# Nineteen attention units with three polynomial tiles in place of four, and the engines' orders written anew

## The chip, the cores and the metric

The kernel runs on one core of a Trainium2 chip, as one launch. The metric is the device time of that launch in microseconds (us). The profile is one execution on the chip, taken by the hardware profiler. A core has five engines that run their own instruction queues: PE (TensorE, matrix products into PSUM), ACT (ScalarE, here the exponentials), DVE (VectorE), POOL (GpSimd) and SP (SyncE, which issues most of the DMAs). Queues meet through semaphores alone, so an engine stands still as soon as the next instruction of its own queue has to wait.

## The reference, cut to what matters

Two independent attention blocks, each on 2,048 rows of 1,024 columns with 32 heads of 32 columns, in bfloat16. Their outputs stand side by side.

```python
def _A_ref(x, wqkv, wo):                    # branch A: full softmax attention
    q, k, v = ...                           # x @ wqkv, split in heads
    scores = einsum('bhqd,bhkd->bhqk', q, k) * Dh ** (-0.5)
    p = softmax(scores)
    o = einsum('bhqk,bhkd->bhqd', p, v)
    return o_joined @ wo

def _B_ref(x, wq, wk, wv, wo, beta):        # branch B: four segments of 512 rows
    for s in range(4):
        p = softmax(qs @ ks.T * scale + mask)   # inside the segment
        a_dot = p @ vs
        a_mem = (phi(qs) @ M) / (phi(qs) @ z + 1e-06)
        o = g * a_mem + (1.0 - g) * a_dot       # g = sigmoid(beta), by head
        M, z = M + phi(ks).T @ vs, z + phi(ks).sum()
    return o_joined @ wo                        # phi(t) = t + 1 if t > 0 else exp(t)
```

## The kernel before

**Units.** Branch A is cut into 64 units: a group of four heads (32 x 4 = 128 partitions) by 256 query rows. A unit has eight sets. A set is four score tiles of 128 x 512 (one for each head, two key blocks by 256 queries), made by PE at L1190 into four PSUM banks (`SLOT_BANKS`: three pairs of banks that rotate). Branch B has 16 units, each a pair of head groups in a segment, with five sets. The B units are dealt out between the A units.

**Exponentials.** A set's four tiles become P, bfloat16 in SBUF. Usually ACT does this with two instructions of 1,024 columns (two banks each), at L1288. So an A unit has 16 exponentials, a B unit ten. `P` is a ring of 20 tiles of 512 columns (`P_RING`). PE then multiplies P with V (L1401) and with a block of ones (L1408), which gives the output and the softmax's sums; DVE turns them (L1515), takes reciprocals (L1518), and POOL multiplies (L1526, L1533).

**Polynomial tiles.** The scores are small, so exp can be had from a parabola. In some sets of a unit the first head's tile does not go to ACT (`plan_cube`): DVE reads the score bank, scales and shifts it into Y (L1236, one of three buffers), POOL squares it into Z (L1245, one of two) and makes Pc from it (L1246, one of three). ACT's first exponential of such a set then has 512 columns in place of 1,024, and the set takes three slots of P in place of four. Which sets those are is said by a digit for each A unit in `POLYS`:

```python
POLYS = "4444444444444444444444444444444444444444444444444444444444444444"
CUBIC = {"3": (0, 2, 4), "4": (0, 2, 4, 6), "5": (0, 1, 2, 4, 6)}
...
        n = 8 * unit[1] + unit[2] if unit[1] < 6 else 48 + PAIR.index(unit[1:])
        return CUBIC[POLYS[n]]
```

The first four units have no polynomial tile, whatever their digit, and the last two have their own entry (`WHOLE`). Branch B uses the same Y, Z and parabola for phi (L1911, then L1245 and L1246, then L1925).

**Jobs.** Beside the units PE has projections (`mm4`, L829): keys, queries and values of later groups and segments, and the output products. `level` spreads them between their release and due times. DVE evicts them from PSUM (L1608) and squares keys and queries (L1621), from which a guard column is made that tells whether the parabola and the unshifted exp may be used; if not, ACT takes another branch of its program (`run_split`).

**Orders.** `schedule` places all operations by a list scheduler with written costs, which gives an order for each engine. `rearrange` then changes these orders by `MOVES`, a string for each engine: "3+2" goes three places on and pulls there the operation that stands two places later. `BANKS` says for each PSUM tenant (projections and sums) whether it lives in bank 6 or 7. Nothing but semaphores sets the time at run time: the written order is what each engine runs.

Of the kernel before, what the change touches and what calls it, by code (L numbers as in the profile page):

```python
# [25 lines left out]
    "666767676767666776766766676667666766676666676666766676666676767677666667666667676677676666766666766676766776766667666766"  # L26
    "666767676776666766667666676667666666666767676776666676666676666766667676677676667666667666666667676677676666766666667676"
    "766767666766667666766667666667666666667676767766666676666676666667676766776766676676666766766776766666766667666666676767"
    "677666676666676667666676667666666667677676676667667666666677676776766666766666667677767666766676676776776667666766667666"
    "66766667666667666677776"  # L30
# [13 lines left out]
POLYS = "4444444444444444444444444444444444444444444444444444444444444444"  # L44
# [101 lines left out]
class Op:  # L146
# [17 lines left out]
    def __hash__(self):  # L164
# [632 lines left out]
class _Kernel:  # L797
# [339 lines left out]
    def cubed(self, unit, part):  # L1137
# [5 lines left out]
        n = 8 * unit[1] + unit[2] if unit[1] < 6 else 48 + PAIR.index(unit[1:])  # L1143
        return CUBIC[POLYS[n]]

# [1139 lines left out]
```

## Time and profile before

| | |
|---|---|
| median of 3 runs | 1058.93 us (1058.56 to 1058.99) |
| profiled execution | 1057.97 us, its span 1056.3 us |
| PE busy | 1023.3 us, 97% of the span |
| ACT busy | 1001.5 us, 95% |
| POOL busy | 724.7 us, 69% |
| DVE busy | 703.4 us, 67% |
| granted TensorE clock | 1.000 |

The span runs from the first to the last instruction of the profile; the profiled execution's own time has 1.7 us around it. In the rows of groups, the text reads: line, engine, operation, what it writes and reads, shapes, count, then busy time in us and the mean of one in ns, then the engine's idle time before these instructions and what ended most of it. In the rows of stretches, each engine has its busy time in us and, in brackets, how many instructions run there; then come the granted clock, the share of the DMA engines and GB/s. In the rows of waits: who waited for whom, the total in us, how often, the longest. Records of successive exponentials overlap somewhat, so a row's mean is longer than the distance from one to the next.

### The profile page before, as it was taken

How to read it: one execution, taken by the hardware profiler on the slowest of the kernel's cores; microseconds unless marked ns; L12 is line 12 of the kernel's file. 1: busy time of each engine (PE TensorE's matmuls, PEld its weight loads, DVE VectorE, ACT ScalarE, POOL GpSimd, SP SyncE). 2: the span in 40 equal slices, each digit the busy share in tenths (PEclk: the TensorE clock that was granted, in tenths of full speed). 3: DMA queues.
4: the chain of work that ended last, by engine and by line, in shares of the span. 5: the costliest groups of instructions: out<-in, count | busy, mean ns of one | idle time of the engine just before them, and what ended most of it. 6: DMA issues, size and time to landing. Idle time of an engine off the chain costs nothing.

```text
span 1056.3 us, 54941 instructions
## 1 busy us (share of the span) xinstructions
PE 1023.3 (97%) x25091; PEld 551.2 (52%) x25092; DVE 703.4 (67%) x1451; ACT 1001.5 (95%) x1193; POOL 724.7 (69%) x999
## 2 busy tenths in 40 slices
PE   9999999999999999999999999999999999999998
PEld 4456455566555454556555445556555445445544
DVE  3457577666656878696755879777646887674444
ACT  5999999999999999898999999999999999999995
POOL 1005567666766888888956899888755878985551
PEclk9999999999999999999999999999999999999999
DMA  9213351007112530033241221133041433122002
GB/s 175 47 43 93 68 138 28 16 13 160 49 41 70 123 85 17 3 62 92 67 113 44 78 65 38 27 75 91 27 113 35 125 102 113 33 68 73 28 29 66
DMA packets 172377, 72.24 MB, mean 68 GB/s; under 512 B 135536, under 2 KB 170352, under 8 KB 172144
## 3 DMA queue, kind: packets, MB, share of 16 engines
q1 hardware_dynamic: 169776, 67.93, 26.3%
q8 instruction: 197, 3.23, 1.3%
q10 hardware_dynamic: 2368, 0.79, 0.3%
q14 instruction: 36, 0.29, 0.1%
HBM read 45.36 MB, written 11.80 MB: 54 GB/s over the span
## 4 chain that ended last, share of the span: by engine, by line
PE 56%; ACT 32%; DVE 4%; POOL 3%; SPq 3%; issue 1%; DMA 0%; ACTq 0%; POOLq 0%; DVEq 0%
ACT P L1288 32%; PE ps L829 27%; PE ps L1190 11%; PE ps L1401 8%; PE ps L1408 8%; SPq L1572 2%; POOL Z L1245 2%; DVE Y L1236 1%; PE ps L1866 1%; PE ps L1638 1%; POOL Pc L1246 1%; DVE T L1515 1%; DMA W_A<-in_A_wqkv_dram 0%; DVE PKQ_B L1925 0%; POOL P L1317 0%
## 5 line engine op out<-in xcount | busy, mean ns | idle before, releaser
L1288 ACT ACTIVATE P<-ps 128x1024 bf16<-128x1024 f32 (+1 forms) x1178 | 991.5, 999 | 33.6 <-PE ps L1190 18.7
L1245 POOL TENSOR_TENSOR Z<-Y 128x512 f32<-128x512 f32 x287 | 304.2, 1062 | 202.2 <-DVE Y L1236 177.7
L1408 PE MATMUL ps<-P,onesb 128*32 128x256 bf16 (+1 forms) x4386 | 300.8, 270 | 0.7 <-issue 0.6
L1401 PE MATMUL ps<-P,V_A 128*32 128x256 bf16 x3618 | 257.7, 274 | 0.7 <-issue 0.3
L1236 DVE TENSOR_SCALAR Y<-ps 128x512 f32<-128x512 f32 x239 | 163.7, 685 | 110.1 <-PE ps L1190 90.5
L1190 PE MATMUL ps<-KQ_A 32*128 32x256 bf16 x4096 | 204.1, 272 | 12.4 <-ACT P L1288 5.5
L1246 POOL TENSOR_SCALAR Pc<-Z 128x512 bf16<-128x512 f32 x239 | 155.6, 654 | 11.0 <-PE ps L1190 0.2
L1190 PEld LDWEIGHTS ps<-KQ_A 32*128 32x128 bf16 x4096 | 62.8, 92 | 163.9 <-ACT P L1288 108.7
L1408 PEld LDWEIGHTS ps<-P,onesb 128*32 128x32 bf16 x4386 | 128.8, 96 | 30.1 <-issue 14.8
L829 PE MATMUL ps<-xT_B,W_B 128*32 128x512 bf16 (+1 forms) x2132 | 138.7, 372 | 0.8 <-DVE OT_B L1948 0.2
L829 PE MATMUL ps<-xT_A,W_A 128*32 128x512 bf16 (+1 forms) x2020 | 131.4, 370 | 2.2 <-DMA W_A<-in_A_wqkv_dram 1.1
L1401 PEld LDWEIGHTS ps<-P,V_A 128*32 128x32 bf16 x3618 | 108.1, 96 | 34.3 <-issue 14.3
L1401 PE MATMUL ps<-Pc,V_A 128*32 128x256 bf16 x478 | 123.1, 273 | 0.4 <-ACT P L1288 0.2
L1408 PE MATMUL ps<-Pc,onesb 128*32 128x256 bf16 x478 | 122.8, 273 | 0.0
L1317 POOL TENSOR_SCALAR_AFFINE_SELECT P<-P 128x768 bf16<-128x768 bf16 (+1 forms) x96 | 76.3, 803 | 34.7 <-ACT P L1288 33.1
L1515 DVE STREAM_TRANSPOSE T<-ps 128x512 f32<-128x512 f32 x122 | 86.3, 708 | 14.0 <-PE ps L1408 11.9
L829 PEld LDWEIGHTS ps<-xT_B,W_B 128*32 128x32 bf16 x2132 | 50.3, 96 | 45.5 <-issue 19.6
L829 PE MATMUL ps<-Wo_B,OT_B 128*32 128x512 bf16 (+1 forms) x1080 | 71.6, 370 | 0.2 <-DVE rc L1518 0.2
L829 PE MATMUL ps<-Wv_B,xT_B 128*32 128x512 bf16 (+1 forms) x1096 | 70.3, 367 | 0.2
L829 PEld LDWEIGHTS ps<-xT_A,W_A 128*32 128x32 bf16 x2020 | 47.4, 96 | 42.1 <-issue 12.5
L1533 POOL TENSOR_TENSOR T<-T,rc 128x256 bf16<-128x256 f32 x74 | 48.9, 663 | 29.6 <-DVE rc L1518 25.8
L1608 DVE CAST KQ_A<-ps 128x512 bf16<-128x512 f32 x60 | 41.3, 689 | 40.5 <-PE ps L829 40.1
(109 smaller groups left out, 1201.0 us busy)
## 6 DMA issues: line engine op xcount, KB each, us to landing
Wv_B<-in_B_wv_dram SPq DMA_DIRECT2D x32, 256.0 KB, 3.5
W_B<-in_B_wk_dram SPq DMA_DIRECT2D x32, 256.0 KB, 3.3
W_B<-in_B_wq_dram SPq DMA_DIRECT2D x32, 256.0 KB, 4.1
Wo_B<-in_B_wo_dram SPq DMA_DIRECT2D x32, 256.0 KB, 3.5
out_dram<-outsb SPq DMA_DIRECT2D x56, 128.0 KB, 1.9
W_A<-in_A_wqkv_dram SPq DMA_DIRECT2D x14, 256.0 KB, 3.6
ot_a_scratch<-OTst SPq DMA_DIRECT2D x52, 64.0 KB, 2.3
xT_A<-ot_a_scratch SPq DMA_DIRECT2D x6, 512.0 KB, 4.8
```

What stands on the lines that cost most here:

```text
L829: ins = e.matmul(out[r], w[:, r], x, start=start, stop=stop, tile_position=(0, 32 * t), skip_group_check=True)
L1190: ins = e.matmul(out, kap, qap, start=st, stop=True, tile_position=(32 * h, 0), skip_group_check=True)
L1236: o = self.dve(lambda e: e.tensor_scalar(Y[:, :], src, SCALE, MID, ALU.mult, ALU.add), 512, key - 9.0, [self.bank[bank]], [rY], fixed=0.15)
L1245: self.pool(lambda e: e.tensor_tensor(Z[:, :], Y[:, :], Y[:, :], ALU.mult), 512, key, [rY], [rZ], rate=0.58)
L1246: return self.pool(lambda e: e.tensor_scalar(dst, Z[:, :], C2, REST, ALU.mult, ALU.add), 512, key, [rZ], [rP], rate=TS_RATE)
L1288: a = self.act(guarded if early and not free else lambda e: e.activation(dst, src, ACT.Exp, scale=SCALE), cols, key, rd, wr, fixed=EXP_FIXED)
L1317: self.pool(lambda e: e.affine_select(v, v, pattern=pat, compare_op=ALU.is_ge, fill=0.0, base=0, channel_multiplier=-1), 2 * nd * P, key + ...
L1401: ins = e.matmul(self.ps[32 * h:32 * h + 32, 512 * obk + q0:512 * obk + q0 + nq], v, p, start=first, stop=last, tile_position=(0, 32 * h), ...
L1408: ins = e.matmul(self.ps[32 * h:32 * h + 32, lcol + q0:lcol + q0 + nq], self.onesb[:, 0:32], p, start=False, stop=last, tile_position=(0, ...
L1515: self.dve(lambda e: e.transpose(T2[:, :], src), 512, k - NORM_K, [obk.res], [ro, rl], fixed=0.17)
L1533: self.pool(lambda e: e.tensor_tensor(half.rearrange("p (b r) -> p b r", r=32), ov, bc, ALU.mult), QC, k, [ro, rr], [rl], rate=0.435)
L1608: self.dve(lambda e: e.tensor_copy(dst, src), 512, key, [self.at(b)], rdst, fixed=0.155)
```

## The change

Nineteen digits of `POLYS` go from 4 to 3: units 22 to 29 (the last two of head group 2 and the first six of group 3), 36 to 43 (the second half of group 4 and the first half of group 5), and 53 to 55. In each of them the set with number 6 no longer has a polynomial tile; its first exponential has 1,024 columns again, and the set takes four slots of P. So there are 19 fewer Y, Z and Pc, and as many exponentials as before, 19 of them longer.

The orders that go with it are replaced as a whole. The strings of `MOVES` have 3,031 moves for PE in place of 3,159, 26 for ACT as before, 1,162 for DVE in place of 1,195 and 722 for POOL in place of 771, and `BANKS` puts 354 of its 503 tenants into bank 6 in place of 359. No other line changes.

```diff
 BANKS = (
-    "666767676767666776766766676667666766676666676666766676666676767677666667666667676677676666766666766676766776766667666766"
+    "666767676767666767766766676667666766676666676666766676666676767767666667666667676767676666766666766676766776766676666766"
...
-POLYS = "4444444444444444444444444444444444444444444444444444444444444444"
+POLYS = "4444444444444444444444333333334444443333333344444444433344444444"
...
 MOVES = {
     "PE": (
-        "14+1 1+2 1+3 5+1 5+1 6+1 1+3 1+1 1+2 4+3 2+1 3+1 1+3 2+1 1+3 1+4 5+1 1+1 1+1 1+1 1+1 1+1 1+1 1+1 1+1 1+1 1+1 1+1 1+1 1+1 "
...
+        "15+1 1+2 1+3 5+1 4+1 6+1 1+3 1+1 1+2 2+2 1+3 1+3 4+1 1+1 1+3 2+1 1+3 1+4 5+1 1+1 1+1 1+1 1+1 1+1 1+1 1+1 1+1 1+1 1+1 1+1 "
...
```

More of the change, by code (lines that the diff above doesn't have):

```diff
@@ L25 @@
 BANKS = (
-    "666767676767666776766766676667666766676666676666766676666676767677666667666667676677676666766666766676766776766667666766"
[L27 to L30, printed above, removed]
+    "666767676767666767766766676667666766676666676666766676666676767767666667666667676767676666766666766676766776766676666766"
+    "667676677676667666667666766676666676667676677676666676666676666667667676767676667666667666677667676677676666766666667676"
+    "766767666766667666766676666677666666676766776766666766676676766666776766776766676666666677766776766666766667676666676767"
+    "676676666766676667666676667666676667676776676667677666666667676776766666766666667677767666766666676776676667666766667666"
+    "66766667666667666677676"
 )
@@ L202 @@
     "PE": (
[109 rows of a table removed]
[105 rows of a table added]
     ),
     "ACT": (
-        "6+1 7+3 24+1 1+1 1+1 1+1 1+1 1+1 1+1 1+1 1+1 1+1 1+1 1+1 1+1 1+1 1+1 52+1 1+1 1+1 1+1 1+1 1+1 1+1 1+1 1083+1 "
+        "6+1 7+3 24+1 1+1 1+1 1+1 1+1 1+1 1+1 1+1 59+1 1+1 1+1 1+1 1+1 1+1 1+1 1+1 1+1 1+1 1+1 1+1 1+1 1+1 1+1 1076+1 "
     ),
     "DVE": (
[40 rows of a table removed]
[39 rows of a table added]
     ),
     "POOL": (
[26 rows of a table removed]
[25 rows of a table added]
     ),
```

342 rows, old and new, of the table MOVES are left out of this document.

## The prediction

> **What bounds the kernel now.** I read the page's busy shares, slices and chain first, then the stage view by units, then the chain and the waits within those stages.
>
> ```profile
> PE 1023.3 (97%) x25091; PEld 551.2 (52%) x25092; DVE 703.4 (67%) x1451; ACT 1001.5 (95%) x1193; POOL 724.7 (69%) x999
> ...
> PE   9999999999999999999999999999999999999998
> DVE  3457577666656878696755879777646887674444
> ACT  5999999999999999898999999999999999999995
> POOL 1005567666766888888956899888755878985551
> ...
> PE 56%; ACT 32%; DVE 4%; POOL 3%; SPq 3%; issue 1%; DMA 0%; ACTq 0%; POOLq 0%; DVEq 0%
> ```
>
> TensorE (PE) and ScalarE (ACT) are both nearly full, and the chain passes between them (56% and 32%). VectorE (DVE) and GpSimd (POOL) average under 70%, but their slices have two humps, at about 350 to 500 and 600 to 730 us. An average says nothing of those, so I cut the trace at unit borders. A unit of branch A has 16 exponentials, a pair of branch B heads ten, and the plan's order tells which exponential opens a unit. The changed units 22 to 29 lie in 362.94 to 497.15 (with two B pairs: 8x16 + 2x10 = 148 exponentials, and two more cut by the ends, the x150 of the row), units 36 to 43 in 596.92 to 725.43, and units 53 to 55 in 878.77 to 928.90 (one pair). I call these I, II and III. The other rows are stretches whose work the change leaves alone.
>
> ```profile
> core 0: us, PE busy (x) PEld busy (x) DVE busy (x) ACT busy (x) POOL busy (x), PEclk, DMA share, GB/s
> 252.85:353.58 100.73, 100.17 (x2432) 51.80 (x2425) 66.82 (x130) 100.57 (x123) 74.66 (x98) 1.00 0.26 72
> 362.94:497.15 134.21, 127.57 (x3328) 71.56 (x3320) 106.57 (x217) 124.86 (x150) 114.38 (x156) 1.00 0.23 49
> ...
> 596.92:725.43 128.51, 124.96 (x3320) 71.17 (x3312) 102.90 (x213) 124.18 (x150) 115.84 (x159) 1.00 0.27 61
> 750.25:816.21 65.96, 65.40 (x1585) 33.98 (x1580) 35.84 (x69) 65.32 (x81) 40.41 (x52) 1.00 0.25 66
> 816.21:878.77 62.56, 60.27 (x1452) 30.14 (x1444) 51.27 (x118) 58.33 (x70) 49.34 (x70) 1.00 0.46 134
> 878.77:928.90 50.13, 48.38 (x1164) 24.52 (x1156) 33.70 (x69) 48.80 (x60) 43.06 (x62) 1.00 0.10 32
> ```
>
> Where POOL is 74% and DVE 66% busy (first row), PE is idle 0.56 us of 100.73 (0.56%) and ACT 0.16. In I, with POOL at 85% and DVE at 79%, PE is idle 6.64 us (4.9%) and ACT 9.35. In II, with POOL at 90% and DVE at 80%, PE is idle 3.55 us (2.8%) and ACT 4.33. In III, with POOL at 86%, PE is idle 1.75 us (3.5%) and ACT 1.33. So in the changed stretches both leading engines lose time, 11.94 us on PE and 15.01 us on ACT, and the side engines are the difference to the first row. The granted clock is 1.00 in each row, so it plays no part.
>
> The chain inside I, II and III, in that order:
>
> ```profile
> by line: ACT P L1288 43.0%; PE ps L829 25.0%; PE ps L1190 9.7%; PE ps L1401 7.8%; PE ps L1408 7.0%; issue 2.5%; DVE T L1515 1.5%; DVE Y L1236 1.4%; PE ps L1638 0.7%; DVE V_B L1608 0.5%; DVE T L1441 0.5%; DVE KQ_B L1608 0.5%; DVE sqB L1621 0
> by line: PE ps L829 28.4%; ACT P L1288 22.5%; PE ps L1190 12.4%; PE ps L1401 8.3%; PE ps L1408 8.2%; POOL Z L1245 3.5%; DVE Y L1236 3.5%; DVE PKQ_B L1925 1.8%; issue 1.6%; DVE sqB L1621 1.5%; POOL P L1317 1.4%; POOL Pc L1246 1.1%; DVE T L15
> by line: PE ps L829 26.9%; ACT P L1288 16.8%; POOL Z L1245 12.7%; PE ps L1190 10.4%; DVE Y L1236 7.0%; PE ps L1401 5.8%; PE ps L1408 4.9%; POOL Pc L1246 3.8%; issue 3.5%; DVE outsb L1608 2.7%; DVE T L1515 1.4%; DVE V_B L1608 1.4%; DVE OT_B
> ```
>
> The polynomial's three steps (Y, Z, Pc) are on the chain: 1.4% of I (Y alone is listed), 8.1% of II, 23.5% of III.
>
> **The change part by part.** The prices:
>
> ```profile
> L1288 ACT ACTIVATE P<-ps 128x1024 bf16<-128x1024 f32 x939 | 913.6, 1085 | 27.8 <-PE ps L1190 13.6 <-PE ps L1408 11.6
> L1245 POOL TENSOR_TENSOR Z<-Y 128x512 f32<-128x512 f32 x287 | 304.2, 1062 | 202.2 <-DVE Y L1236 177.7 <-DVE Y L1911 5.8 <-DVE flags L1718 3.9
> L1236 DVE TENSOR_SCALAR Y<-ps 128x512 f32<-128x512 f32 x239 | 163.7, 685 | 110.1 <-PE ps L1190 90.5 <-PE ps L829 7.3 <-POOL Z L1245 6.1
> L1288 ACT ACTIVATE P<-ps 128x512 bf16<-128x512 f32 x239 | 158.1, 661 | 5.7 <-PE ps L1190 5.1
> L1246 POOL TENSOR_SCALAR Pc<-Z 128x512 bf16<-128x512 f32 x239 | 155.6, 654 | 11.0 <-PE ps L1190 0.2
> ```
>
> *Added.* One tile a unit moves to ACT: no new instruction, but one of 512 columns becomes one of 1,024, 1,085 - 661 = 424 ns more. That is 19 x 0.424 = 8.06 us of ACT time: 3.39 in I, 3.39 in II, 1.27 in III. What hides it is ACT's idle time of 9.35, 4.33 and 1.33 us; without that cover it costs 8.06. I take the share that ACT has of the chain in each stretch: 0.430 x 3.39 + 0.225 x 3.39 + 0.168 x 1.27 = 1.46 + 0.76 + 0.21 = 2.4 us. The bounds are 0 and 8.06.
>
> *Removed.* 19 Y of 685 ns, 13.0 us of DVE, and 19 pairs of Z and Pc of 1,062 + 654 ns, 32.6 us of POOL. Of the chain, the steps make 0.014 x 134.21 + 0.081 x 128.51 + 0.235 x 50.13 = 1.9 + 10.4 + 11.8 = 24.1 us, and one tile in four goes: -6.0 us. What is late next is a PE projection or the norm's transpose (T L1515, 1.5% of I). This supposes that the chain's tiles go in proportion. The bounds are nothing (the removed sets, each unit's fourth, were not the late ones) and PE idle falling to the first row's 0.56% of 312.85 us, 1.75 us: a gain of 11.94 - 1.75 = 10.2.
>
> *Moved buffers.* A set without a polynomial tile takes four slots of the ring of 20 P tiles and not three, so an exponential overwrites a slot somewhat sooner after its readers. The wait that would grow is the second of these (ACT's waits in I):
>
> ```profile
> ACT P L1288 <- PE ps L1190: 6.4, 10, 1.2
> ACT P L1288 <- PE ps L1408: 2.4, 4, 1.2
> ```
>
> In I, 8 slots come on top of some 8x(4x4 + 4x3) + 2x20 = 264, 3%; 3% of 2.4 us is under 0.1 us, and I count nothing. Its cover is PE's lead on the softmax products; gone, each such wait would cost up to 1.2 us. The reverse effect, on the ring of three Pc tiles, is a gain that I also leave out.
>
> *Moved orders.* The order lists of PE, DVE and POOL are written anew for the whole kernel (3,031 PE moves for 3,159), and the bank string with them. PE's work is the same matmuls. The cost can be on either side of zero: untouched stretches have PE idle from 0.85% (750.25 row) to 3.7% (816.21 row). I take zero, since no row favours a sign, and give the spread to a rival.
>
> The sum is 2.4 - 6.0 = -3.6 us. A second way to it: with 13.7 us of POOL's work gone from I and II each and 5.1 from III, POOL would stand at 75% to 80% of the present lengths, between the first row (74%, 0.56% idle) and I to III together (273.28 of 312.85, 87%, 3.8% idle). A straight line at 77% gives 1.2%, 3.9 us, a gain of 8.0; with the 2.4 us of ACT, -5.6. I stay near the first, as less idle time on ACT couples the two engines more tightly: -3.8. The profiled run took 1057.97 us (span 1056.3, 1.7 around it), so 1054.2; the median of the runs, 1058.93, lies 0.96 above that run, so 1055.1.
>
> **The rivals.** *ACT takes over (slower).* In I to III ACT keeps its present idle time, since it waits for the QK products (6.4 us in I) that PE brings as late as before, and every added 424 ns lengthens the stretch: +8.06, 1067.0. It decides as soon as more than 6.0 of the 8.06 us, three quarters, lie on the chain, or as soon as the relief is hidden. For it: ACT's 43% of the chain in I, and the B pairs between, where ACT hardly pauses. Against it: in I and II ACT still has idle time to absorb more than it gets.
> The Trainium skill (Trainium Kernel Development and Optimization, Performance Expectations) says that matmul busy time is a bad metric of TensorE's closeness to its roofline, and that weight-load busy time tells it. By that rule TensorE, with 52% in PEld, has room, the 95% of ACT is the bound, and this rival would be the case; the chain's 56% on PE speaks against it.
>
> *The new order loses elsewhere (slower).* About 743 us keep their work but not their order. Were two stretches like the first row's 100.73 us to go from 0.56% to the 816.21 row's 3.7% PE idle, that is +6.3 us, past the gain: 1061.4. For it: such a stretch exists with no polynomial more. Against it: the same 33 us of PE idle in all leave as much to win.
>
> *Nothing left.* Chain steps change places: the fourth tile of a unit is the one with the most slack, half the relief comes (-3), and ACT costs as much. 1057 to 1061.
>
> **How the numbers follow.** Forecast 0.47, ACT takes over 0.20, the order loses 0.17, nothing left 0.16. A measurement here tells about 0.2%, 2.1 us, from no change (the three runs lie within 0.43 us; orders add their scatter). Faster is then 0.47, within it 0.16, slower 0.37. The forecast's own range is 1049 (gain of 10) to 1056.8. For 8 in 10 the range goes from 1050, short of the relief's full bound, to 1066, just short of the whole ACT price on the path.
>
> **What would show it.** Right: 1,024-column exponentials up by 19 and 512-column ones down to 220; Y 220, Z 268; POOL under 80% in I, II and III; PE idle there below 9 us in all; Y, Z, Pc down to less than a tenth of the chain in III; I and II shorter. Wrong: ACT's share of the chain in II over 40% with the lengths grown (the first rival); I to III shorter but the stretches between longer (the second); or PE idle in I to III still 12 us although POOL fell, which would mean that POOL and DVE were not its cause.

## The result and the profile after

The changed kernel takes 1062.25 us in the median of 13 runs (1060.79 to 1065.79), the kernel before 1058.44 us beside it (13 runs). The ratio is 1.0042 with a 95% interval of 1.0031 to 1.0052: 4.4 us slower, where 3.8 us faster was forecast. The time lies inside the stated range of 1050 to 1066, but on the other side of before. The profiled span grew from 1056.3 to 1059.4 us.

The head of the changed kernel's page (its line numbers are six smaller than before, so L1282 is the exponential that was L1288):

```profile
span 1059.4 us, 55091 instructions
...
PE 1024.9 (97%) x25211; PEld 555.0 (52%) x25212; DVE 688.2 (65%) x1432; ACT 1008.1 (95%) x1193; POOL 690.7 (65%) x961
...
POOL 1005668666766777767947777876766787875542
...
PE 67%; ACT 25%; DVE 4%; POOL 1%; SPq 1%; DMA 1%; issue 1%; ACTq 0%; DVEq 0%; POOLq 0%
```

The side engines got their relief: POOL 34.0 us less, DVE 15.2 us less, ACT 6.6 us more. PE neither gained nor stood still less. The groups, by shape:

```profile
L1282 ACT ACTIVATE P<-ps 128x1024 bf16<-128x1024 f32 x958 | 926.9, 1082 | 26.6 <-PE ps L1184 12.2 <-PE ps L1402 10.6 <-PE ps L823 1.5
L1239 POOL TENSOR_TENSOR Z<-Y 128x512 f32<-128x512 f32 x268 | 283.8, 1063 | 224.1 <-DVE Y L1230 195.5 <-DVE Y L1905 12.6 <-DVE bias L1704 4.5
L1230 DVE TENSOR_SCALAR Y<-ps 128x512 f32<-128x512 f32 x220 | 150.6, 685 | 99.7 <-PE ps L1184 94.2 <-POOL Z L1239 2.0 <-PE ps L823 1.2
L1282 ACT ACTIVATE P<-ps 128x512 bf16<-128x512 f32 x220 | 144.6, 657 | 3.2 <-PE ps L1184 2.9
```

Counts and prices are as foreseen: 19 exponentials longer, 19 Y and 19 Z fewer, at the same mean times. The stretches, cut at the same exponentials (the second, fourth and sixth rows are I, II and III):

```profile
0.00:362.97 362.97, 354.61 (x8567) 196.30 (x8572) 216.64 (x476) 344.69 (x409) 198.66 (x281) 1.00 0.35 73
362.97:498.36 135.39, 128.03 (x3324) 71.50 (x3316) 100.29 (x210) 127.93 (x150) 102.14 (x143) 1.00 0.27 59
498.36:598.13 99.77, 98.35 (x2392) 51.36 (x2388) 68.27 (x139) 97.12 (x117) 71.63 (x97) 1.00 0.25 66
598.13:731.49 133.36, 128.24 (x3356) 72.25 (x3352) 99.72 (x208) 127.08 (x149) 102.39 (x143) 1.00 0.29 62
731.49:881.61 150.12, 146.24 (x3524) 74.56 (x3519) 105.58 (x220) 146.38 (x175) 109.82 (x152) 1.00 0.36 97
881.61:931.34 49.73, 48.45 (x1208) 25.82 (x1204) 32.32 (x67) 49.65 (x60) 38.78 (x58) 1.00 0.10 33
931.34:1059.40 128.06, 120.96 (x2884) 63.20 (x2876) 65.33 (x118) 115.30 (x141) 67.28 (x90) 1.00 0.17 53
```

The partner rows of before that the prediction did not show:

```profile
0.00:362.94 362.94, 354.62 (x8515) 194.73 (x8520) 221.67 (x477) 345.52 (x409) 199.83 (x281) 1.00 0.34 76
497.15:596.92 99.77, 97.66 (x2328) 49.64 (x2320) 66.85 (x136) 97.00 (x117) 74.30 (x100) 1.00 0.27 69
725.43:878.77 153.34, 149.58 (x3640) 77.51 (x3632) 105.46 (x224) 146.09 (x176) 109.25 (x153) 1.00 0.34 96
928.90:1056.30 127.40, 120.52 (x2844) 62.12 (x2840) 66.28 (x121) 115.09 (x141) 68.03 (x92) 1.00 0.17 54
```

I is 1.18 us longer, II 4.85 longer, III 0.40 shorter. The stretch behind II is 3.22 shorter, but that is work moved forward: II has 36 matmuls more and 3.3 us more PE time, its follower 116 fewer and 3.3 us less. POOL fell to 75% in I and 77% in II, and yet PE stands idle 7.36, 5.12 and 1.28 us in the three, 13.8 us where it was 11.9. This is the last of the outcomes that the prediction named as wrong: POOL's load fell and PE's idle time did not. The first rival's sign did not come: ACT has 24.0% of the chain in II (22.5% before), not over 40%. One sign of being right did come. The chain of III, which had 23.5% of Y, Z and Pc:

```profile
by line: ACT P L1282 83.4%; POOL Z L1239 4.2%; POOL PKQ_B L1240 2.4%; POOL OT_B L1522 1.3%; POOL T L1520 1.2%; POOL Pc L1240 1.2%; POOL rc L1514 1.2%; DVE Y L1230 1.2%; issue 0.9%; DVE T L1521 0.9%; PE ps L1395 0.8%; PE ps L1184 0.7%; DVE Y
```

They have 6.6% of it now (Z 4.2, Y 1.2, Pc 1.2). That is 8.5 us less of the chain, and yet III is only 0.40 us shorter, with 1.27 us added on ACT.

Who keeps PE waiting at the QK products shows a part of the reason. Two rows of the waits of before, then the same two of the changed kernel (total us, times, longest):

```profile
PE ps L1190 <- ACT P L1288: 7.7, 21, 0.8
PE ps L1190 <- DVE Y L1236: 3.7, 9, 0.8
```

```profile
PE ps L1184 <- ACT P L1282: 11.2, 28, 1.2
PE ps L1184 <- DVE Y L1230: 1.0, 4, 0.3
```

A set's QK products need PSUM banks that both DVE's Y and ACT's exponentials must have left. The waits for Y went down by 2.7 us, and the waits for ACT went up by 3.5. These are one profile each: in the profiles of later runs that leave the polynomial work as it was, the wait for Y lies between 2.1 and 4.0 us.

### The profile page after: what moved, and what is told of

It reads as the page before. It is cut to its first block, busy times and chain, and to the rows that moved or that the text cites. A ratio compares the mean times of both kernels' runs of the same rounds, so it can differ in the third digit from the quotient of the medians.

```text
span 1059.4 us, 55091 instructions
## 1 busy us (share of the span) xinstructions
PE 1024.9 (97%) x25211; PEld 555.0 (52%) x25212; DVE 688.2 (65%) x1432; ACT 1008.1 (95%) x1193; POOL 690.7 (65%) x961
## 4 chain that ended last, share of the span: by engine, by line
PE 67%; ACT 25%; DVE 4%; POOL 1%; SPq 1%; DMA 1%; issue 1%; ACTq 0%; DVEq 0%; POOLq 0%
PE ps L823 33%; ACT P L1282 25%; PE ps L1184 13%; PE ps L1395 10%; PE ps L1402 9%; PE ps L1860 1%; SPq L1566 1%; DVE Y L1230 1%; DVE T L1509 1%; PE ps L1632 1%; DMA PKt_B<-PKQ_B 1%; POOL Z L1239 1%; ACT P L1260 0%; DVE KQ_B L1602 0%; DMA xT_A<-in_A_x_dram 0%
## 5 line engine op out<-in xcount | busy, mean ns | idle before, releaser
L1282 ACT ACTIVATE P<-ps 128x1024 bf16<-128x1024 f32 (+1 forms) x1178 | 998.3, 1003 | 29.8 <-PE ps L1184 15.0
L1239 POOL TENSOR_TENSOR Z<-Y 128x512 f32<-128x512 f32 x268 | 283.8, 1063 | 224.1 <-DVE Y L1230 195.5
L1230 DVE TENSOR_SCALAR Y<-ps 128x512 f32<-128x512 f32 x220 | 150.6, 685 | 99.7 <-PE ps L1184 94.2
L1240 POOL TENSOR_SCALAR Pc<-Z 128x512 bf16<-128x512 f32 x220 | 143.8, 659 | 9.4
L1395 PE MATMUL ps<-Pc,V_A 128*32 128x256 bf16 x440 | 112.8, 274 | 0.3 <-POOL Pc L1240 0.3
L1402 PE MATMUL ps<-Pc,onesb 128*32 128x256 bf16 x440 | 112.7, 273 | 0.0
L1602 DVE CAST outsb<-ps 128x512 bf16<-128x512 f32 x56 | 38.7, 690 | 50.6 <-PE ps L823 23.1
L823 PEld LDWEIGHTS ps<-xT_A,W_A 128*32 128x32 bf16 x2040 | 47.6, 96 | 42.8 <-issue 12.6
```

The source lines that it names most:

```text
L823: ins = e.matmul(out[r], w[:, r], x, start=start, stop=stop, tile_position=(0, 32 * t), skip_group_check=True)
L1230: o = self.dve(lambda e: e.tensor_scalar(Y[:, :], src, SCALE, MID, ALU.mult, ALU.add), 512, key - 9.0, [self.bank[bank]], [rY], fixed=0.15)
L1239: self.pool(lambda e: e.tensor_tensor(Z[:, :], Y[:, :], Y[:, :], ALU.mult), 512, key, [rY], [rZ], rate=0.58)
L1240: return self.pool(lambda e: e.tensor_scalar(dst, Z[:, :], C2, REST, ALU.mult, ALU.add), 512, key, [rZ], [rP], rate=TS_RATE)
L1282: a = self.act(guarded if early and not free else lambda e: e.activation(dst, src, ACT.Exp, scale=SCALE), cols, key, rd, wr, fixed=EXP_FIXED)
L1395: ins = e.matmul(self.ps[32 * h:32 * h + 32, 512 * obk + q0:512 * obk + q0 + nq], v, p, start=first, stop=last, tile_position=(0, 32 * h), ...
```

## The experiments

All comparisons are with the kernel before on the same chip, unless said otherwise; us are the ratio's difference times 1058. Most runs keep the order of before to the instruction and change the size of the work in the nineteen sixth sets, by this helper:

```python
def sixth(t):     # the set that the change takes the polynomial tile from
    if t["kind"] != "A" or t["part"] is not None or t["set"][3] != 6 or t["unit"] in WHOLE:
        return False
    g, c = t["unit"][1:]
    return NINETEEN[8 * g + c if g < 6 else 48 + PAIR.index((g, c))] == "3"   # NINETEEN = the new POLYS
```

**The change taken apart: relief alone, ScalarE's time alone, both.** Relief:

```diff
+        n = 8 if sixth(t) else 512
-            o = self.dve(lambda e: e.tensor_scalar(Y[:, :], src, SCALE, MID, ALU.mult, ALU.add)
+            o = self.dve(lambda e: e.tensor_scalar(Y[:, 0:n], src, SCALE, MID, ALU.mult, ALU.add)
...          # Z and Pc likewise on [:, 0:n]
```

> The kernel before with its order of work unchanged, in which Y, Z and Pc of the sixth set of the nineteen units work on 8 columns in place of 512 (those tiles' values are left out): the relief of VectorE and GpSimd alone. The forecast's theory (side engines hold up TensorE): 6 us faster than before, TensorE idle in the three stretches down from 11.9 to about 6 us. Rival ACT (only ScalarE's time counts): within 1 us of before. Rival order (the new order lost the time): within 2 us of before, nothing lost.

ScalarE's time (in `plan_exp`):

```diff
                 dst = Pt.rearrange("p b n -> p (b n)")
+                if lo and sixth(take[0]):
+                    src = src.unsqueeze(1).to_broadcast([P, 2, 512])
+                    dst = Pt.bitcast(dt.uint8).rearrange("p a (b n) -> p (a b) n", b=2)
```

> The kernel before with its order unchanged, in which the 512-column exponential of the sixth set of the nineteen units reads its scores twice and so has 1,024 columns (its values are left out, written as bytes): ScalarE's added time alone, 8.06 us. The forecast's theory: 2.4 us slower than before. Rival ACT: 6 to 8 us slower. Rival order: at most 2 us slower.

Both edits together:

> Both edits on the kernel before, order unchanged: the change's work in the old order (the sixth set's values are left out). The forecast's theory: 3.6 us faster than before. Rival ACT: as slow as the changed kernel or slower, 4 to 8 us over before. Rival order: within 2 us of before, so that the 3.8 us of the changed kernel come with its order.

Measured: relief alone 0.9992 (0.9982 to 1.0002), 0.8 us faster at best guess and not told from nothing; ScalarE's time alone 1.0048 (1.0033 to 1.0063), 5.1 us slower; both 1.0039 (1.0025 to 1.0053), 4.1 us slower. The two parts add up, 5.1 - 0.8 = 4.3, and the change's work in the old order costs what the changed kernel costs (4.4). So, as far as these intervals tell, the loss comes with the work and not with the new order, which brought nothing back either.

The waits of PE at QK, in the relief run, then with ScalarE's time added, then with both:

```profile
PE ps L1200 <- ACT P L1299: 9.2, 26, 0.8
...
PE ps L1200 <- DVE Y L1247: 1.7, 5, 0.8
```

```profile
PE ps L1200 <- ACT P L1301: 11.6, 34, 0.8
PE ps L1200 <- DVE Y L1246: 2.1, 5, 0.8
```

```profile
PE ps L1200 <- ACT P L1302: 12.2, 37, 0.8
...
PE ps L1200 <- DVE Y L1247: 1.3, 3, 0.8
```

With relief alone the wait for Y falls by 2.0 us and the wait for ACT rises by 1.5. As the order is the same, the traces can be compared instruction by instruction. Of the nine QK products that waited for Y in before, three no longer wait (0.34, 0.48 and 0.62 us), one falls from 0.29 to 0.13 us, one waits for ACT instead (0.46 us where it was 0.45), and four still wait for Y; a wait for Y of 0.28 us is new. So ACT, the other reader of the banks, took over one wait in nine. Of its 1.5 us more, 0.5 lie in unit 1, long before the first changed unit, and show in the run with the cut (below) as well. I, II and III in the relief run:

```profile
362.63:495.28 132.65, 127.45 (x3328) 71.69 (x3320) 99.08 (x217) 124.37 (x150) 105.16 (x156) 1.00 0.25 51
595.08:722.85 127.77, 124.89 (x3324) 71.24 (x3316) 99.47 (x214) 124.06 (x150) 107.01 (x160) 1.00 0.29 62
876.18:926.07 49.89, 48.38 (x1164) 24.50 (x1156) 32.00 (x69) 48.79 (x60) 39.28 (x62) 1.00 0.10 32
```

PE is idle 9.6 us there, where it was 11.9 and the forecast's theory expected about 6. The three are 2.5 us shorter in this profile, which caught the fastest of the twelve runs (1055.14 us); their median gives the 0.8.

With ScalarE's time alone, the same comparison shows where the price arises. PE's idle time grows by 4.2 us. Of these, 2.7 us lie at QK products of the set behind the lengthened exponential's (set 7), which start 0.06 to 0.14 us after that exponential's end where they have to wait. Another 1.4 us lie at QK products of branch B, 0.9 of them 1.9 us after such an end.

**The changed kernel without the added time.**

```diff
+                if take[0]["h"] == 0 and sixth(take[0]):
+                    src, dst = self.ps[:, c0 + 512:c0 + 1024], Pt[:, 1, :]
```

> The changed kernel with its own order, in which the first exponential of the sixth set of the nineteen units does 512 columns in place of 1,024 (the first head's tile is left out there): ScalarE's added time taken back, the relief kept. The forecast's theory: 2.4 us faster than the changed kernel, about 1060. Rival ACT: 6 to 8 us faster than the changed kernel, 1054 to 1056. Rival order: 1 to 2 us faster than the changed kernel, still slower than before.

Measured 1.0026 (1.0016 to 1.0036), 1.7 us below the changed kernel and still 2.8 over before. This is what the rival of the order expected (the forecast's 2.4 us is not excluded, with about 1.1 us either way on both), and it does not fit ScalarE as the bound: 8 us taken from it in an order fitted to the longer exponentials give back a fifth. Taking away is not the mirror of adding, so the next runs did both in the old order.

**Less of ScalarE's time, and the same in other units.** The other units, 8 to 21 and 45 to 49, are called light.

```diff
+                if lo and sixth(take[0]):
+                    src, dst = src[:, 0:64], dst[:, 0:64]
```

> The kernel before, order unchanged, with the first exponential of the sixth set of the nineteen units on 64 columns in place of 512 (the second head's tile is left out there but for 64 columns): 19 x 0.373 = 7.1 us less of ScalarE's time in the same places where 8.06 us more cost 5.1. ScalarE as the bound: 4 to 5 us faster. Lockstep theory (what is added to either engine passes on, what is taken from one alone meets the other's work): 0.5 to 2.5 us faster.

> The same lengthening by 8.06 us of ScalarE's time as before, order unchanged, in nineteen other units, 8 to 21 and 45 to 49, where VectorE and GpSimd have room and ScalarE has almost no idle time (the sixth set's values are left out). If ScalarE's idle time in the nineteen units of the change covered part of its price: 7 to 8 us slower here against 5.1 there. If the cover plays no part: 5 us as there. The forecast's theory by shares of the chain: under 5 us, as the chain there lies mostly on TensorE.

> The 64-column cut, 7.1 us less of ScalarE's time, in those other nineteen units, order unchanged (the second head's tile left out there but for 64 columns). ScalarE as the bound there (it is idle 0.2% of the time): 6 to 7 us faster. Lockstep theory (TensorE is as full there): 0 to 1.5 us faster.

Measured: the cut in the change's places 0.9996 (0.9987 to 1.0005); the lengthening in the light units 1.0047 (1.0035 to 1.0060), 5.0 us; the cut in the light units 0.9992 (0.9983 to 1.0001). Where 8.06 us more cost 5.1, 7.1 less gain 0.4: ScalarE is not the bound that one could shorten. ACT's waits for QK in the kernel before, then with the cut in the change's places, show where the cut went:

```profile
ACT P L1288 <- PE ps L1190: 18.7, 37, 1.2
```

```profile
ACT P L1300 <- PE ps L1200: 22.9, 52, 1.2
```

ACT waits for PE 52 times in place of 37, 4.2 us more. And the price of the added time is the same 5 us in units where ACT hardly ever stands idle, so its idle time in I to III covered nothing as a total.

**How much hangs on the side engines at all.** Against the relief run:

```diff
-        n = 8 if sixth(t) else 512
+        n = 8 if t["unit"][1] else 512
```

> The kernel before, order unchanged, with Y, Z and Pc of all polynomial tiles from head group 1 on (223 of 239) on 8 columns in place of 512 (their values are left out): nearly all of the polynomial work gone from VectorE and GpSimd. The forecast's theory (their steps make 24 us of the chain in the three stretches): 20 us or more faster. Lockstep theory (TensorE and ScalarE alternate in a written order, the side engines have slack, their chain steps are filled by the next thing at once): 2 to 6 us faster. If the 19 tiles' 0.8 us scale with the count: 9 us faster.

Measured 0.9947 (0.9933 to 0.9960), 5.6 us for nearly the whole polynomial work. The forecast had 6.0 us for 19 tiles of it. I, II and III in this run:

```profile
364.29:497.49 133.20, 127.10 (x3328) 71.42 (x3320) 82.22 (x217) 124.23 (x150) 73.16 (x156) 1.00 0.23 49
597.16:724.16 127.00, 124.80 (x3324) 71.04 (x3316) 80.45 (x214) 123.48 (x150) 76.03 (x160) 1.00 0.28 63
876.87:926.32 49.45, 48.22 (x1164) 24.42 (x1156) 27.40 (x68) 48.56 (x59) 26.70 (x61) 1.00 0.10 32
```

POOL is down to between 54% and 60%, and PE is still idle 9.5 us of the 11.9.

**Where idle time does cover.** After these runs it stood open why 15 us of ScalarE's idle time hid so little.

```diff
+GAPS = (410, 412, 439, 469, 470, 495, 497, 527, 528, 533, 535, 537, 695, 743, 745, 775, 803, 1024, 1035)
...
+                if len(self.exps) in GAPS:      # the exponential's number in the kernel
+                    m = 3 - lo
+                    src = self.ps[:, c0:c0 + 512].unsqueeze(1).to_broadcast([P, m, 512])
+                    dst = Pt.bitcast(dt.uint8).rearrange("p a n -> p (a n)")[:, 0:512 * m].rearrange("p (b n) -> p b n", n=512)
```

> The kernel before, order unchanged, with 512 columns more (8.06 us of ScalarE's time in all) on nineteen exponentials of the three stretches behind which ScalarE stood idle for 0.46 to 1.35 us in the profile (their values are left out, written as bytes). If idle time covers only what lies directly ahead of it: 0 to 1.5 us slower than before. If an exponential's end holds up TensorE by the banks that it releases, whatever ScalarE does next: 4 to 5 us slower, as in the change's places. The forecast's theory by chain shares: 2.4 us.

Half the dose in the change's own places (against the run of ScalarE's time):

```diff
-                    src = src.unsqueeze(1).to_broadcast([P, 2, 512])
+                    src = src[:, 0:256].unsqueeze(1).to_broadcast([P, 3, 256])
...          # dst likewise, 768 columns
```

> The kernel before, order unchanged, with 256 columns more in place of 512 on the sixth sets' first exponential of the nineteen units (4.0 us of ScalarE's time; the values are left out). A price in proportion: 2.5 us slower than before. A threshold (each place has some slack that the first 0.2 us use up): under 1 us.

Measured: 1.0004 (0.9995 to 1.0013) with the time put ahead of the idle times, nothing that can be told from before; 1.0018 (1.0009 to 1.0027) for half the dose, 1.9 us, about four tenths of the full price. The same 8.06 us in the same three stretches cost 5.1 us in one set of places and 0.4 in another. I, II and III, first with the time in the change's places, then ahead of the idle times:

```profile
363.43:498.85 135.42, 127.91 (x3327) 71.62 (x3321) 106.16 (x218) 126.96 (x150) 114.99 (x157) 1.00 0.24 50
599.00:729.64 130.64, 125.55 (x3316) 71.16 (x3308) 102.44 (x213) 127.12 (x149) 116.49 (x159) 1.00 0.27 60
884.13:935.28 51.15, 48.62 (x1164) 24.59 (x1156) 34.32 (x69) 50.05 (x59) 43.08 (x62) 1.00 0.10 32
```

```profile
363.13:497.03 133.90, 127.74 (x3328) 71.52 (x3320) 105.80 (x217) 129.65 (x149) 114.81 (x156) 1.00 0.23 50
596.84:725.37 128.53, 124.93 (x3320) 71.06 (x3312) 102.95 (x213) 126.31 (x149) 116.06 (x159) 1.00 0.27 61
878.95:929.31 50.36, 48.42 (x1164) 24.50 (x1156) 33.94 (x69) 49.66 (x59) 43.14 (x62) 1.00 0.10 32
```

In the second fence I and II are as long as before (134.21 and 128.51), ACT is busier, and its idle time, 4.25 us in I where it was 9.35, has been used up. In the first fence ACT is still idle 8.46 us in I: it waits at the places where it waited, and the stretch is longer. Directly behind the nineteen exponentials of the second fence, ACT's idle time went from 12.3 us to 4.7.

Single places can be read from these traces too, as the order is that of before: how much later than in before the twelfth exponential behind a changed one starts, beyond the delay that the changed one already had at its own start. A full dose is 0.43 us. At six places all of it arrives (within 0.02 us), at nine places 0.05 to 0.27 us of it are swallowed, at three 0.35 us or more, and at one the delay grows to 0.89. Of the half dose (0.21 us) at most 0.06 arrives at eleven places and 0.10 to 0.21 at seven; at one the later exponential starts 0.38 us earlier than in before. After the cut (0.37 us) the later exponential starts where it did, within 0.05 us, at 14 of the 19 places, and between 0.84 us earlier and 0.16 later at the others.

**The plan's own order.**

```diff
-BANKS = ( ... )
+BANKS = ""
-MOVES = { ... }
+MOVES = {}
```

> The kernel before with the list scheduler's own order: no MOVES, and every PSUM tenant of the jobs in bank 6 and the sums in bank 7. It is the partner of a_plain. All theories: well slower than before, by 1% or more, since the written moves are gone.

> The changed kernel in the same way, no MOVES and no bank string: the nineteen digits alone in an order that nobody fitted to either load. Lockstep theory (ScalarE's added time passes on, the relief does not): 3 to 7 us over b_plain. The forecast's theory: below b_plain by 3 to 6 us. Rival order (the new search came out worse): equal to b_plain within 2 us.

Measured 1.0450 (1.0437 to 1.0463) and 1.0433 (1.0419 to 1.0446), 47.6 and 45.8 us over before. With the nineteen digits the plan's order is 1.8 us faster if anything, and the intervals meet. Neither the forecast nor the lockstep expectation of 3 to 7 us slower held there; the rival's, equal within 2 us, did. So the work's price of 4 us belongs to the written order. I suppose that in an order 47 us looser the added time finds room; no run shows this. The written moves are worth ten times the change on either side.

**The splits.** Projections come in halves of 256 columns, which run as one step where they are neighbours in the order.

```diff
+        for o in [o for o in q if o.twin is not None]:
+            i, j = q.index(o), q.index(o.twin)
+            if j != i + 1:
...
+                    q.insert(i + 1, q.pop(j))
```

> The changed kernel with every split projection step joined again: where the order has put other work between the two 256-column halves of a step, the second half follows the first, and both become one step of 512 columns. The changed kernel has 30 more such splits than before and TensorE 1.6 us more busy time. If the splits are part of its loss: 1 to 6 us faster than the changed kernel. If they fill gaps that would stand empty otherwise: within 1 us or slower.

> The same joining on the kernel before, whose order has 95 splits. If a split costs TensorE 53 ns (1.6 us for 30) and nothing else hangs on it: 5 us faster than before, a version that beats both. If the halves fill gaps: within 1 us of before or up to 2 us slower.

Measured 1.0052 (1.0040 to 1.0064) for the changed kernel, no better than its 1.0042, and 1.0017 (1.0008 to 1.0026) for before, 1.8 us slower. So joining gains nothing, and the 30 splits more of the changed kernel are not its loss; that the halves fill gaps fits this. No version here that does the whole work beats before.

## Why the prediction was wrong

*The relief (-6.0 us) was the step that failed most.* It measured -0.8 (-1.9 to 0.2). I took the time of Y, Z and Pc on the chain, 24.1 us, and let a quarter go. A chain is followed back to whoever came last. The 24.1 us are the length of that path, and tell nothing of how long PE stood still at its end: the waits of before show 3.7 us for Y in all, at nine QK products. Three of them went with the relief (1.4 us), and one (0.45 us) passed to ACT, the other reader of the banks. The second way to the sum failed as well: POOL's load is for the most part not what kept PE idle, since with POOL at 54% to 60% in I to III PE was still idle 9.5 of 11.9 us there. With nearly the whole polynomial work gone, 5.6 us are to be had.

*ScalarE's price (2.4 us) was mis-sized.* It measured 5.1 (3.5 to 6.7), against the bounds of 0 and 8.06. Two things were wrong in the step. The share of the chain does not price an addition: in the light units it was mostly PE's, and the price was 5.0 all the same. The chain of the prediction's first row, which holds part of them, names no ACT among its larger shares:

```profile
by line: PE ps L829 46.7%; PE ps L1190 18.6%; PE ps L1401 14.1%; PE ps L1408 13.4%; DVE PKQ_B L1925 1.4%; DVE KQ_A L1608 1.4%; DVE sqA L1621 0.9%; issue 0.8%; DVE T L1426 0.6%; PE ps L1638 0.6%; DVE KQ_B L1608 0.6%; DVE Y L1236 0.6%; DVE OT
```

And I named ACT's idle time in the stretch as cover, as a sum; the run with the time ahead of the idle times shows that it covers what ends right before it.

*Moved buffers and order at zero held, taken together.* The old order with the new work and the old buffers gave 4.1 us, the new order with the new buffers 4.4. As the intervals are 1.1 and 1.5 us wide either way, a part of that size may hide there, and the two were not told apart.

*The rivals.* "ACT takes over" came nearest in sign and mechanism, since the relief proved hidden and most of the 8.06 us lay on the path, but as a bound it fails: ACT shortened by 7.1 us in the same places gives 0.4 us, whose interval reaches from 1.4 us faster to 0.5 slower. What the runs show is narrower. PE and ACT hand the PSUM banks to each other in a written order. A longer exponential makes the next set's QK late, and behind it, in PE's queue, everything else: with ScalarE's time alone, 4.1 of PE's 4.2 us of new idle time lie at QK products of set 7 and of branch B. After a shorter one ACT waits for PE, which is no sooner done. "The new order loses elsewhere" falls with the run of both edits: 4.1 us without any new order. "Nothing left" was right in that the relief came out smaller than the chain's share, but it had 3 us for each part, where 0.8 and 5.1 were measured.

The Trainium skill (Trainium Kernel Development and Optimization, Performance Expectations) holds matmul busy time to be a bad metric. The trace agrees in this much: with ScalarE's time added, the same 25,091 matmuls show 1025.4 us of PE busy time where before shows 1023.3 (one profile each), so some waiting seems to be counted as work.

```profile
PE 1025.4 (96%) x25091; PEld 551.5 (52%) x25092; DVE 703.1 (66%) x1451; ACT 1008.5 (95%) x1193; POOL 726.6 (68%) x999
```

The reading that the prediction took from it, that the engine at 95% is then the bound, the runs do not bear out.

That half the dose costs 1.9 us, the whole 5.1 and a cut nothing follows from the slack that each place has, between none and 0.4 us (above). What stays open is why the new order, written with the new work, brought nothing back, and why the same work costs nothing in the plan's order.

## What to carry to other kernels

Here idle time hid added work where it directly followed that work, and a stretch's total of idle time was no cover; the trace says which instructions have a gap behind them. Before a chain's share is counted as gain, look up how long the leading engine stood still at the end of that path, and who else the waiting instruction needs (here the second reader of the same banks). In these written orders additions cost most of their length and nearly equal removals gave next to nothing, so price both with a run that changes one size and keeps the order.

## What the runs showed of the hardware beyond that

ScalarE, 95% busy, had work to lose without a gain, and so had the two side engines: 7.1 us less on ScalarE, and in the relief run 13.0 us less on VectorE (690.4) with 24.1 less on GpSimd (700.6), each moved the time by under 1 us. A 512-column exponential repeated to 1,024 columns and written as bytes cost ScalarE what the change's 1,024-column ones do: both kernels show ACT at 1008 us.
